# The last output half of a decode kernel, summed as 16 rows of 128 columns

## The chip, the cores and the metric

The kernel runs on one core of a Trainium2 chip. The metric is the device time of one execution in microseconds (us), lower is better. Before the change three runs took 1340.95, 1341.06 and 1341.16 us; the median is 1341.06.

## The reference

One decode step for 4 sequences: attention over a cache of 8192 positions with 32 heads of 128, its output projection, a gated feed-forward part, and a gate that mixes the two. With one position per sequence and one chosen row, what is computed is this:

```python
g = sigmoid((x * gate_w).sum(-1))
q = (x @ wq).reshape(4, 32, 128)
p = softmax(einsum("bhd,bhkd->bhk", q, k_cache) * 128 ** -0.5)
a = einsum("bhk,bhkd->bhd", p, v_cache).reshape(4, 4096) @ wo
y = ((silu(x @ w_gate) * (x @ w_up)) @ w_down) * sigmoid(x @ w_r)
b = x + y
out = g * a + (1 - g) * b
```

The caches hold 4 x 32 x 8192 x 128 bf16 values each; `wo` is 4096 x 1024, and `out` is 4 x 1024 in bf16. Everything that the change touches belongs to `... @ wo` and the sum with `(1 - g) * b`.

## The kernel before

All inputs stream through one ring of SBUF (`flat`), loaded by DMAs that SP issues in the order of the program. The order of the stages is written out by hand (`order` and the loop behind it): the query projection, then the gate and up projections beside the first K loads, then pairs of K and V steps (32 each, four heads a step), with a softmax per group of eight steps. PE, DVE and POOL keep the order of the program; each waits on semaphores and nothing overtakes on its engine.

When the last K step is done, the PSUM space of the scores is freed and two banks `acc0` and `acc1` are opened in it: the two halves of the output, 512 columns each. `acc(0)` is partitions 0 to 3 of the first, `acc(1)` partitions 32 to 35 of the second. `mm_acc` (L296) adds a product to one of them. The down projection (`wd_piece`) and `x` times its weight (`add_x`, an f32 matmul with the 4x4 diagonal `dg`) go in first, and the output projection last.

The output projection takes `wo` in eight blocks `g` of 512 rows; a block lies on 128 partitions with `FR` = 4 rows each, so a block is 4 x 2 matmuls (row `r`, half `n`), each with `LT[:, r, g, :]` (128x4) as weights and 512 columns of `wo` streaming. `LT` is the attention output, turned by `o_rows` (matmuls with an identity, L428, and a DVE copy, L430): blocks 0 to 5 ahead of the last V step, blocks 6 and 7 behind it. `wo_two` and `wo_block` issue the loads of `wo` on SP and return the function that does the products.

Behind the last V step the list `last` is worked off: blocks 1 and 2, the final sums of that step, block 3, `o_rows` for blocks 6 and 7, then blocks 4, 5, 6, and block 7. Block 7 is loaded in pieces (`cuts`): rows 0 and 1 (512 KB), row 2 (256 KB), row 3's first half and row 3's second half (128 KB each). Then DVE evicts `acc(0)` (L694) and SP stores it (L695); ScalarE evicts `acc(1)` (L696) and stores it from its own queue (L697).

`turned` hands out one of two staging tiles `TB` in turn. `Zt` are two tiles of 128 x 4 x 160 bf16 in which POOL lays the query for the K steps (`spread`); after the last K step nothing uses them. `o_ps` are the two PSUM tiles in which the V steps sum; after the last one they are free. `PB` holds the softmax weights, spread by ScalarE and POOL (L568, L570).

## Time and profile before

| what | value |
|---|---|
| median of three runs | 1341.06 us |
| span of the profiled execution | 1339.2 us |
| PE busy (share of the span) | 1031.3 us (77%) |
| DVE busy | 638.7 us (48%) |
| ACT busy | 57.7 us (4%) |
| POOL busy | 67.0 us (5%) |
| moved by DMA | 576.14 MB, mean 430 GB/s |
| chain that ended last, by engine | DMA 67%, PE 22%, DVE 9% |
| idle time of PE ahead of `acc` matmuls of `wo`, until a load | 2.8 us in four waits |

The span runs from the first instruction of the program to the last on this core; the time of a run holds what lies around it too. A busy share is an average over stages; the chain of waits, followed back from the last instruction, tells which of them set the end in each stage. An engine's name with a q (SPq, ACTq) is its queue issuing DMAs. PE means matmuls, PEld the loading of their weights.

### The profile page before, as it was taken

How to read it: one execution, taken by the hardware profiler on the slowest of the kernel's cores; microseconds unless marked ns; L12 is line 12 of the kernel's file. 1: busy time of each engine (PE TensorE's matmuls, PEld its weight loads, DVE VectorE, ACT ScalarE, POOL GpSimd, SP SyncE). 2: the span in 40 equal slices, each digit the busy share in tenths (PEclk: the TensorE clock that was granted, in tenths of full speed). 3: DMA queues.
4: the chain of work that ended last, by engine and by line, in shares of the span. 5: the costliest groups of instructions: out<-in, count | busy, mean ns of one | idle time of the engine just before them, and what ended most of it. 6: DMA issues, size and time to landing. Idle time of an engine off the chain costs nothing.

```text
span 1339.2 us, 6936 instructions
## 1 busy us (share of the span) xinstructions
PE 1031.3 (77%) x4654; PEld 139.8 (10%) x1486; DVE 638.7 (48%) x385; ACT 57.7 (4%) x58; POOL 67.0 (5%) x174
## 2 busy tenths in 40 slices
PE   2386787887777788777787977777797778687887
PEld 0011000001010010101001110100111011111111
DVE  2285998556553436555352556634345556100001
ACT  0000000100010000100010000100000000110000
POOL 2000000100010000100010000100001000100000
PEclk9697998898888998888889988888998889689999
DMA  9999999999999999999999999999999999999998
GB/s 415 433 437 437 435 437 435 420 438 433 433 435 437 427 433 435 429 438 431 433 431 433 435 439 427 429 433 435 438 430 428 433 429 429 438 429 445 422 422 352
DMA packets 13032, 576.14 MB, mean 430 GB/s; under 512 B 1436, under 2 KB 1700, under 8 KB 1970
## 3 DMA queue, kind: packets, MB, share of 16 engines
q1 hardware_dynamic: 12994, 575.69, 99.6%
q8 instruction: 24, 0.39, 0.1%
q14 instruction: 6, 0.05, 0.0%
q10 hardware_dynamic: 8, 0.00, 0.0%
HBM read 575.68 MB, written 0.01 MB: 430 GB/s over the span
## 4 chain that ended last, share of the span: by engine, by line
DMA 67%; PE 22%; DVE 9%; POOL 0%; ACT 0%; issue 0%; SPq 0%
DMA ring<-in_A_k_cache_dram 53%; PE S_ps L516 15%; DMA ring<-in_A_v_cache_dram 10%; DVE ring L511 9%; PE o_ps L587 5%; DMA ring<-in_B_w_gate_dram 3%; DMA ring<-in_A_wo_dram 2%; PE o_ps L342 1%; POOL PB L570 0%; DVE mx L536 0%; PE led L633 0%; ACT TB L545 0%; PE acc L296 0%; POOL Z L492 0%; PE o_ps L633 0%
## 5 line engine op out<-in xcount | busy, mean ns | idle before, releaser
L511 DVE STREAM_TRANSPOSE ring<-ring 128x2048 uint32<-128x2048 uint32 x256 | 566.5, 2276 | 307.7 <-DMA ring<-in_A_k_cache_dram 307.7
L516 PE MATMUL S_ps<-ring,Z 128*128 128x512 bf16 x2048 | 519.9, 408 | 229.3 <-DVE ring L511 216.1
L587 PE MATMUL o_ps<-ring,PB 128*64 128x512 bf16 x2048 | 457.4, 384 | 35.7 <-DMA ring<-in_A_v_cache_dram 33.3
L516 PEld LDWEIGHTS <-Z 128*128 128x128 bf16 x512 | 53.0, 104 | 683.0 <-issue 683.0
L617 DVE SCALAR_TENSOR_TENSOR OS<-o_ps,mE,OS 128x512 f32<-128x512 f32 x33 | 24.8, 751 | 161.7 <-ACT OS L613 160.2
L587 PEld LDWEIGHTS <-PB 128*64 128x64 bf16 x512 | 56.7, 111 | 428.3 <-issue 427.6
L625 DVE SCALAR_TENSOR_TENSOR OS<-o_ps,mE,OS 128x512 f32<-128x512 f32 x5 | 3.7, 750 | 143.6 <-ACT OS L623 143.6
L492 POOL COPY Z<-qa 32x4 bf16<-32x4 bf16 x128 | 25.8, 201 | 716.7 <-PE S_ps L516 689.6
L570 POOL COPY PB<-PT 32x1024 bf16<-32x1024 bf16 (+3 forms) x23 | 33.4, 1452 | 466.6 <-PE o_ps L587 360.7
L613 ACT ACTIVATE OS<-o_ps,mE 128x512 f32<-128x512 f32 x11 | 7.6, 687 | 671.2 <-PE o_ps L587 671.2
L568 ACT COPY PB<-PT 32x1024 bf16<-32x1024 bf16 (+3 forms) x21 | 30.3, 1444 | 22.4 <-PE o_ps L587 17.4
L545 ACT ACTIVATE TB<-S_ps,mx 128x2048 bf16<-128x2048 f32 x4 | 7.9, 1967 | 321.7 <-DVE mx L542 321.7
L254 PE MATMUL S_ps<-identb,x 6*128 6x6 bf16 x8 | 0.6, 196 | 22.3 <-DMA x<-in_gate_w_dram 22.3
L342 PE MATMUL o_ps<-ring,xw 128*4 128x512 bf16 (+2 forms) x128 | 12.9, 490 | 3.5 <-DMA ring<-in_B_w_gate_dram 3.5
L633 PEld LDWEIGHTS o_ps<-selg,OS 128*128 128x128 f32 x88 | 11.5, 191 | 8.8 <-issue 8.5
L550 DVE STREAM_TRANSPOSE PT<-TB 128x2048 bf16<-128x2048 bf16 x4 | 9.2, 2312 | 6.4 <-ACT TB L545 6.4
L296 PE MATMUL acc<-ring,hT 128*4 128x512 bf16 x54 | 7.9, 466 | 5.5 <-DMA ring<-in_B_w_down_dram 5.5
L536 DVE TENSOR_REDUCE mx<-S_ps 128x1 f32<-128x2048 f32 x4 | 9.1, 2282 | 6.0 <-PE S_ps L516 6.0
L296 PE MATMUL acc<-ring,LT 128*4 128x512 bf16 x64 | 8.8, 378 | 3.3 <-DMA ring<-in_A_wo_dram 2.8
L633 PE MATMUL o_ps<-selg,OS 128*128 128x8 f32 x88 | 10.5, 245 | 0.0
L623 ACT ACTIVATE OS<-o_ps,mE 128x512 f32<-128x512 f32 x5 | 3.4, 687 | 151.2 <-PE o_ps L587 151.2
L256 DVE COPY xw<-S_ps 128x48 bf16<-128x48 bf16 x1 | 0.2, 184 | 17.5 <-PE S_ps L254 17.5
(83 smaller groups left out, 88.4 us busy)
## 6 DMA issues: line engine op xcount, KB each, us to landing
ring<-in_A_v_cache_dram SPq DMA_DIRECT2D x7, 4096.0 KB
ring<-in_A_k_cache_dram SPq DMA_DIRECT2D x6, 4096.0 KB, 33.9
ring<-in_A_v_cache_dram SPq DMA_DIRECT2D x6, 2048.0 KB, 28.9
ring<-in_B_w_gate_dram SPq DMA_DIRECT2D x1, 7168.0 KB
ring<-in_B_w_up_dram SPq DMA_DIRECT2D x1, 7168.0 KB
ring<-in_B_w_down_dram SPq DMA_DIRECT2D x1, 6912.0 KB
ring<-in_A_wo_dram SPq DMA_DIRECT2D x2, 2048.0 KB
ring<-in_A_wo_dram SPq DMA_DIRECT2D x3, 1024.0 KB, 34.5
```

The costliest lines, as they stand in the source:

```text
L296: nc.tensor.matmul(acc(n), lhsT=lhsT, rhs=rhs, start=start, stop=True, skip_group_check=True)
L342: nc.tensor.matmul(ps[32 * k:32 * k + Bn, z, :].rearrange("p (f r) -> p f r", r=FR)[:, :, lo:hi], lhsT=xT[TW * half + t], rhs=rhs, start=( ...
L492: nc.gpsimd.tensor_copy(out=Z[at, :, QP - 1 + QP * q], in_=qa[at, :, h0 + q, b])
L511: nc.vector.transpose(out=kn[:, half], in_=kn[:, half])
L516: nc.tensor.matmul(sps[:, z, :], lhsT=Z[:, 2 * half + e, s:s + P], rhs=T[:, half, 16 * z:16 * z + 16, :, e], start=(t + k + half + e == 0) ...
L536: nc.vector.tensor_reduce(out=mx[:, 0:1], in_=sps[:].rearrange("p z n -> p (z n)"), axis=AX.X, op=ALU.max)
L550: nc.vector.transpose(out=PT[:].rearrange("p j i -> p (j i)"), in_=PTs)
L568: nc.scalar.copy(out=Bv[at, :, :, q, :], in_=Pv[at])
L570: nc.gpsimd.tensor_copy(out=Bv[at, :, :, q, :], in_=Pv[at])
L587: nc.tensor.matmul(o_ps[w // 2][row:row + NM, w % 2, :], lhsT=PB[:, RD * (d % NW) + n, z].rearrange("p w s j -> p (w s j)"), rhs=vn[:, j0 ...
L617: nc.vector.scalar_tensor_tensor(out=OS[:], in0=o_ps[w // 2][:, w % 2, :], scalar=mE[:, w:w + 1], in1=OS[:], op0=ALU.mult, op1=ALU.add)
L633: nc.tensor.matmul(oT, lhsT=OS[:, q * Dh:(q + 1) * Dh], rhs=selg[:, q].rearrange("p t s -> p (t s)"), start=(q == 0), stop=(q == 3), skip_ ...
```

## The change

Three things change.

1. In the last block (7), the second output half is not added to `acc(1)` as one matmul of 4 x 512, but as four of 16 x 128 into a new place `fine`: partitions 0 to 15 of `o_ps[0]`, 128 columns. Row 4s + b of `fine` holds columns 128s to 128s + 127 of the half for sequence b. The weights for it are padded: `LP` has, for every row and every s, 128x16 weights that are zero but for the four columns of `LT` at 4s. What `acc(1)` has gathered up to block 6 is brought over by `acc_to_fine`: ScalarE copies it to SBUF as f32, and four f32 matmuls with padded 4x16 identities (`EP`) put it into `fine`. `LP` and `EP` lie in the two `Zt` tiles, which POOL clears again (`fine_weights`).
2. Block 7 is cut in another way: rows 0 and 1; the first half of rows 2 and 3; the second half of row 2; the second half of row 3. The first half is thus complete two pieces before the end.
3. The ends change engines: ScalarE evicts the first half and stores it from its queue; DVE evicts `fine` (16x128), and SP stores it, with the columns put back in place by the store's pattern.

```diff
+    SEG = P
+    NS = NB // SEG
+    SW = NS * Bn
...
         nc.vector.tensor_copy(out=LT[:, :, g0:g1, :], in_=lp)
+        if g1 == NWB:
+            nc.vector.tensor_copy(out=LP.rearrange("p r (s q) -> p r s q", s=NS)[:, :, :, 0:Bn],
+                                  in_=LT[:, :, NWB - 1, :].unsqueeze(2).to_broadcast([P, FR, NS, Bn]))
...
-        elif half is None:
+        elif half is not None:
+            cols = slice(half * NB, (half + 1) * NB)
+            nc.sync.dma_start(out=w[:, r0:r1, cols], in_=wov[:, g, r0:r1, cols])
+        else:
             nc.sync.dma_start(out=w[:, r0:r1].rearrange("p r n -> p (r n)"),
                               in_=wov[:, g, r0:r1].rearrange("p r n -> p (r n)"))
-        else:
-            nc.sync.dma_start(out=w[:, r0, half * NB:(half + 1) * NB], in_=wov[:, g, r0, half * NB:(half + 1) * NB])
...
                 for n in range(NH) if half is None else [half]:
-                    mm_acc(n, LT[:, r, g, :], w[:, r, n * NB:(n + 1) * NB])
+                    if n == 0 or g < NWB - 1:
+                        mm_acc(n, LT[:, r, g, :], w[:, r, n * NB:(n + 1) * NB])
+                        continue
+                    for s in range(NS):
+                        nc.tensor.matmul(fine, lhsT=LP[:, r, SW * s:SW * (s + 1)], rhs=w[:, r, NB + SEG * s:NB + SEG * (s + 1)],
+                                         start=False, stop=True, skip_group_check=True)
         return use
...
+    LP, EP = [z[:].rearrange("p e w -> p (e w)") for z in Zt]
+    LP = LP[:, 0:FR * NS * (SW + Bn)].rearrange("p (r w) -> p r w", r=FR)
+    EP = EP[:, 0:2 * NS * (SW + Bn)].bitcast(F32)
+    fine = o_ps[0][0:SW, 0, 0:SEG]
+
+    def fine_weights():
+
+        for z in Zt:
+            nc.gpsimd.memset(z[:], 0.0)
+        nc.gpsimd.tensor_copy(out=EP[0:Bn].rearrange("p (s q) -> p s q", s=NS)[:, :, 0:Bn],
+                              in_=ident[0:Bn, 0:Bn].unsqueeze(1).to_broadcast([Bn, NS, Bn]))
+
+    def acc_to_fine():
+
+        a = turned(Bn, NB, F32)
+        nc.scalar.copy(out=a, in_=acc(1))
+        for s in range(NS):
+            nc.tensor.matmul(fine, lhsT=EP[0:Bn, SW * s:SW * (s + 1)], rhs=a[:, SEG * s:SEG * (s + 1)],
+                             start=(s == 0), stop=True, skip_group_check=True)
...
                 add_x()
+                fine_weights()
...
-    cuts = [(g, 0, FR) for g in range(4, NWB - 1)] + [(NWB - 1, 0, 2), (NWB - 1, 2, 3)] + [(NWB - 1, FR - 1, FR, n) for n in range(NH)]
+    cuts = [(g, 0, FR) for g in range(4, NWB - 1)] + [(NWB - 1, 0, 2), (NWB - 1, 2, FR, 0), (NWB - 1, 2, 3, 1), (NWB - 1, 3, FR, 1)]
...
-    for use in last:
+    for i, use in enumerate(last):
+        if i == len(last) - 4:
+            acc_to_fine()
         use()
-    res = [turned(Bn, NB, lo=32 * n) for n in range(NH)]
-    nc.vector.tensor_copy(out=res[0], in_=acc(0))
-    nc.sync.dma_start(out=out2[:, 0:NB], in_=res[0])
-    nc.scalar.copy(out=res[1], in_=acc(1))
-    nc.scalar.dma_start(out=out2[:, NB:D], in_=res[1])
+    res = [turned(Bn, NB), turned(SW, SEG)]
+    nc.scalar.copy(out=res[0], in_=acc(0))
+    nc.scalar.dma_start(out=out2[:, 0:NB], in_=res[0])
+    nc.vector.tensor_copy(out=res[1], in_=fine)
+    nc.sync.dma_start(out=out2[:, NB:D].rearrange("b (s c) -> s b c", c=SEG), in_=res[1])
```

## The prediction

> **What bounds the kernel now.** I read the page first, then the chain of waits in order of time for the last 100 us, then the timeline of the last 7 us, and last the groups by shape for prices. The page:

> ```profile
> span 1339.2 us, 6936 instructions
> PEclk9697998898888998888889988888998889689999
> DMA  9999999999999999999999999999999999999998
> ```

> The DMA engines are busy in every slice but a part of the last one, so the loads set the time, and the change moves no byte of them except in how the last 0.5 MB is cut. What it can move is what lies behind the last load. The chain of waits, its end:

> ```profile
> 1311.27 24.05 DMA ring<-in_A_wo_dram
> 1335.32 0.04 issue
> 1335.36 1.05 PE acc L296 x4
> 1336.41 0.02 issue
> 1336.43 0.58 ACT TB L696
> ```

> Up to 1335.32 a load holds the chain, then four matmuls (1.05 us), then ScalarE's eviction of the second half (0.58 us). The timeline of the end (start, length, engine, line, operation, count, idle time before it):

> ```profile
> 1333.46 1.03 PE L296 MATMUL acc<-ring,LT 128*4 128x512 bf16 x8 [1.44 <-DMA ring<-in_A_wo_dram]
> 1334.70 0.60 PE L296 MATMUL acc<-ring,LT 128*4 128x512 bf16 x4 [0.22 <-DMA ring<-in_A_wo_dram]
> ...
> 1335.70 0.69 PE L296 MATMUL acc<-ring,LT 128*4 128x512 bf16 x2
> 1336.12 0.68 DVE L694 CAST TB<-acc 4x512 bf16<-4x512 f32 x1 [6.49 <-PE acc L296]
> 1336.43 0.58 ACT L696 CAST TB<-acc 4x512 bf16<-4x512 f32 x1 [10.90 <-PE acc L296]
> 1336.83 0.29 SPq L695 DMA_DIRECT2D out_dram<-TB  x1
> 1337.04 0.55 ACTq L697 DMA_DIRECT2D out_dram<-TB  x1
> ```

> Block 6 ends at 1334.49 (1333.46 + 1.03). The first cut of block 7 (rows 0 and 1, four matmuls) starts when its load lands, 1334.70; row 2 follows at 1335.36, row 3's first half at 1335.70, its second half at 1336.02 (1335.70 + 0.69 - 0.38), each on landing. PE idles between them: the loads, not PE, hold this end. The span ends at 1339.17, 2.13 us after ScalarE began its store (1337.04).

> **The change, part by part.** All times are on this execution's clock; its span is 1339.2 and the median of the runs 1341.06, so about 1.9 us lie around the span, and I add the change of the span to 1341.06.

> *Prologue of the fine sums.* `fine_weights` puts two memsets and a 4x4x4 copy on POOL behind the spread of the last softmax group. The rows: 625 ns for a memset of Z, some 200 for a copy, 1.45 us in all. POOL finished that spread at 1148.42 and next works at 1177.28 (its timeline), so 27 us of POOL's idle time hide it:

> ```profile
> 1143.54 4.88 POOL L570 COPY PB<-PT 32x768 bf16<-32x768 bf16 x3 [75.46 <-DVE PT L550]
> 1177.28 1.28 POOL L570 COPY PB<-PT 32x256 bf16<-32x256 bf16 x2 [28.86 <-PE o_ps L587]
> ```

> If that cover were gone, the PB copies and with them the V matmuls would be 1.45 us late. The copy of LT into LP is a small DVE operation of 64 elements per lane, about 0.2 us by the 32- and 96-element copies below, after 1329.63; it is wanted after 1335. Nothing on the path.

> *The wait that is added.* `acc_to_fine` stands in PE's order between block 6 and block 7. ScalarE can copy acc(1) only when block 6 is done, and PE can't start the four f32 matmuls before that copy; everything of block 7 is queued behind them on PE, the first half's matmuls too. ScalarE itself has nothing else to do there (10.90 us idle). So: 1334.49 + 0.03 (as from 1336.41 to 1336.43) + 0.58 (row of the same 4x512 shape) + 0.05 (as 1335.32 to 1335.36, and a little for the signal) = 1335.15 at which PE goes on. That is 0.45 us after it goes on now, and the loads no longer hold it.

> *Four f32 matmuls of 128 columns.* The nearest rows:

> ```profile
> L296 PE MATMUL acc<-TB,dg 4*4 4x512 f32 x4 | 1.0, 587 | 0.0
> L355 PE MATMUL S_ps<-identb,TB 128*128 128x128 bf16 x8 | 0.8, 220 | 1.6 <-DVE TB L351 1.3 <-DVE qT L356 0.3
> L360 PE MATMUL S_ps<-qT,R 128*128 128x128 bf16 x4 | 0.5, 260 | 0.3 <-DVE qT L356 0.3
> L430 DVE CAST LT<-led 128x96 bf16<-128x96 f32 x1 | 0.3, 258 | 12.3 <-PE led L428 12.3
> L430 DVE CAST LT<-led 128x32 bf16<-128x32 f32 x1 | 0.2, 191 | 0.9 <-PE led L428 0.9
> ```

> Two f32 multiplications of 512 columns leave four records of 587 ns, in two pairs 0.43 us apart (1.02 in all less 0.59). So a record streams 512 columns in 0.43 us, 128 in 0.107, and a multiplication has two records. Whether the two of a pair were the halves of one multiplication or the two column groups (0:4 and 32:36) this can't tell: 4 x 0.107 = 0.43 us if halves overlap, 8 x 0.107 = 0.86 if not. I take 0.86, since all four now use one column group and a stream can't share it. PE at 1336.01. [...]

> *Block 7's products.* Today each row's two matmuls overlap, being in two column groups (eight in 1.03 us). The fine sums sit on partitions 0 to 15, the group of acc(0), so nothing overlaps any more. A 512-column matmul alone in its group takes 0.215 us (the first row below: 16 in 3.61 us, less one of 0.38, by 15). A weight load and a matmul of 128 columns: four of L355, whose weights are even larger, take 0.40 us in the window below, with 0.22 for one, so 0.06 each; L360's four give 0.08 ((0.5 - 0.26) / 3), the upper end.

> ```profile
> 1321.05 3.61 PE L587 MATMUL o_ps<-ring,PB 128*64 128x512 bf16 x16 [1.28 <-DMA ring<-in_A_v_cache_dram]
> ...
> 31.10:31.50 0.40, 0.40 (x4) 0.28 (x5) 1.00 0.00 0
> ```

> The first cut: 2 x (0.215 + 4 x 0.06) = 0.91, to 1336.92. Rows 2 and 3 of the first half: 0.43, to 1337.35; the last of them began at 1337.13 and is done 0.38 later, at 1337.51. The second half of rows 2 and 3: 8 x 0.06 = 0.48; the last pair starts at 1337.77 and is done 0.22 later, at 1337.99. All the loads are down before, so their new cut (the first half of rows 2 and 3 in 256 pieces of 1 KB, where row 2 was 128 of 2 KB) costs nothing here; a tenth of a us if PE were waiting for it.

> [...]

> *First half out.* ScalarE in place of DVE: 1337.51 + 0.03 + 0.58 = 1338.12, store begun 1338.15, and by today's 2.13 from there the span would end at 1340.28.

> *Second half out.* DVE evicts 16x128 in place of 4x512. From the two L430 rows, 67 ns for 64 elements: 128 elements are 0.29 us, less than today's 0.58 on ScalarE. 1337.99 + 0.03 + 0.29 = 1338.31, store begun by SP at 1338.34. SP's queue has only this store and the closing waits in it. SP's issue is 0.26 us shorter, but its data came as late after the start as ScalarE's (within 0.04 us: pieces up to 1337.73 and up to 1337.98 in the slices of DMA traffic), so 2.09. The store has 16 pieces of 256 B where it had 4 of 1 KB. Today's four begin 0.04 us apart; 12 more at that pace are 0.48, spread over engines that take them side by side 0. I take 0.1, nearer to the lower end, since the first load of the kernel has its sixteen engines begin within 0.3 us (0.02 each). End: 1338.34 + 2.09 + 0.1 = 1340.53.

> *Sum.* 1340.53 - 1339.17 = +1.36 us: PE's last matmul is done 1.59 later (1337.99 against 1336.40), the eviction gives back 0.29, the queue 0.04, the small pieces take 0.1. 1341.06 + 1.36 = 1342.4 us. A measurement of this kernel tells about 0.2% (2.7 us) from no change, so this counts as no change, though slower.

> **The rivals.**

> *Hidden (1340.7).* If PE were through the copy, the f32 sums and the first cut before the last load lands, only the shorter end would remain: 0.29 + 0.04 less 0.1 for the pieces, the final four pairs about as long as the matmul of 0.38 (3 x 0.06 + 0.22 = 0.40). So 0.2 to 0.3 us faster. For it: PE does idle there today. Against it: its idle time between block 6 and row 3's second half is about 0.8 us, and the added work is 0.66 of waiting, 0.86 of f32 and the lost overlap; PE would be ready for the last piece at 1337.59, 1.57 us after it lands (1336.02).

> *f32 halves overlap (1342.0).* All as above with 0.43 for the four matmuls.

> *Small things are dearer (1343.1).* The fine pairs take L360's 0.08 (16 x 0.02 = 0.32) and the 16 pieces of the store 0.48 (0.38 more than taken).

> *The clock falls (slower, 1344.9).* PE would now stand still from 1334.49 to 1335.15. If that cost it the granted clock, all its streams behind the wait (0.86 + 0.91 + 0.43 + 0.48 = 2.68 us) would double, on top of the 1.36: about +4.0, less what no stream is. It decides from 1.3 us more upward. For it: earlier slices show a granted clock of 6 and 7 tenths where PE waits for loads. Against it: the clock of the last windows is 1.00 (column behind the busy times), over an idle time of 1.44 us ahead of 1333.46, longer than this one:

> ```profile
> 1333.00:1334.50 1.50, 1.03 (x8) 0.34 (x8) 0.00 (x0) 0.00 (x0) 0.00 (x0) 1.00 0.68 256
> 1334.50:1335.30 0.80, 0.60 (x4) 0.17 (x4) 0.00 (x0) 0.00 (x0) 0.00 (x0) 1.00 0.50 174
> ```

> That the edit doesn't do what it says hardly arises: PE's order in the built program has the four f32 matmuls behind block 6 and four matmuls per row in place of one.

> **How the numbers follow.** The forecast as summed 0.68 (its own range 1341.9 to 1342.8); f32 overlapping 0.13; small things dearer 0.11; hidden 0.04; the clock 0.04. The range: below, 1341.8 if all low ends come together, and half a us on towards the hidden case where PE had part cover, 1341.3; above, the dear case and 0.2 for the difference between executions, 1343.3. The hidden case is within 0.2%, so faster by more has 0.01; the clock, and an end dearer than any row, make 0.06 slower by more; 0.93 remains for no change.

> **What would show it.** Right: a gap on PE behind block 6 that ScalarE's copy ends; eight f32 records after it, 0.8 to 0.9 us; no later wait of PE for a load; DVE's 16x128 eviction of 0.3 us last in the chain, with the end of the span some 1.4 us later. Wrong: PE waiting for a load at the last cut (hidden), f32 records in overlapping pairs, a granted clock under 1.00 behind 1334, or a span that differs before 1333, which nothing here explains.

## The result, and the profile after

The changed kernel took 1344.71 us (median of nine executions, 1342.92 to 1345.68), the kernel before beside it 1341.20 (1340.95 to 1341.97). The ratio is 1.0022, with a 95% interval of 1.0012 to 1.0031: slower by about 3 us (1.6 to 4.2), where 1342.4 was forecast and 1341.3 to 1343.3 was the range. The nine executions are two groups: four from 1342.92 to 1343.44, five from 1344.71 to 1345.68. The profiled one, 1343.01, is of the lower group, and its span is the page's first line:

```profile
span 1341.0 us, 6980 instructions
```

The end of its chain of waits (start, length, what):

```profile
1301.37 31.93 DMA ring<-in_A_wo_dram
1333.30 0.04 issue
1333.34 1.05 PE acc L300 x8
1334.39 0.02 issue
1334.41 0.58 ACT TB L479
1335.00 0.04 issue
1335.04 1.04 PE o_ps L481 x8
...
1337.48 0.46 PE o_ps L459 x8
1337.94 0.02 issue
1337.97 0.28 DVE TB L732
```

Before, a load held this chain up to 1335.32. Now the last load in it is the one ahead of block 6 (1333.30); from there on it is PE, ScalarE's copy (L479), the f32 matmuls (L481), block 7 and the eviction of `fine` (L732), without a gap. Behind that stand the stores, in the timeline:

```profile
1338.13 0.54 ACTq L731 DMA_DIRECT2D out_dram<-TB  x1
1338.27 0.75 SPq L733 DMA_DIRECT2D out_dram<-TB  x1
```

SP's store of the 16 rows takes 0.75 us to issue, where its store of 4 rows took 0.29. From its start to the end of the span it is 2.7 us (1341.0 - 1338.27).

So the lower group is the forecast with a dearer store. The upper group needed experiments.

### The profile page after: what moved, and what is told of

It reads as the page before. It is cut to its first block, busy times and chain, and to the rows that moved or that the text cites. A ratio compares the mean times of both kernels' runs of the same rounds, so it can differ in the third digit from the quotient of the medians.

```text
span 1341.0 us, 6980 instructions
## 1 busy us (share of the span) xinstructions
PE 1033.3 (77%) x4674; PEld 141.6 (11%) x1506; DVE 638.5 (48%) x386; ACT 58.3 (4%) x59; POOL 68.1 (5%) x177
## 4 chain that ended last, share of the span: by engine, by line
DMA 68%; PE 21%; DVE 10%; ACT 0%; issue 0%; SPq 0%; DVEq 0%
DMA ring<-in_A_k_cache_dram 52%; PE S_ps L549 15%; DVE ring L544 10%; DMA ring<-in_A_v_cache_dram 8%; DMA ring<-in_A_wo_dram 5%; PE o_ps L620 4%; DMA ring<-in_B_w_gate_dram 3%; PE o_ps L346 1%; DVE OS L650 0%; DVE mx L569 0%; ACT TB L578 0%; PE acc L300 0%; PE led L666 0%; PE o_ps L481 0%; PE o_ps L459 0%
```

## The experiments

The lines called "filling products" are `fill(n, g)`: n matmuls of 128x128 by 512 columns over block g's weights of `wo`, already loaded, into a bank of `o_ps[1]` that nothing reads any more.

**1. The changed kernel again**, no edit.

> The changed kernel again, unaltered, for a second profile and more executions. What is open is the spread: nine executions lay between 1342.9 and 1345.7, in two groups near 1343.2 and 1345.0, while the profiled one of 1343.0 is explained to 0.2 us by its end (PE done 1.5 later, store 0.6 dearer). Theory A (clock): in some executions TensorE runs its last 2.7 us of streams at half the granted clock; then a profile of a 1345 execution shows a granted clock of 0.5 behind 1334 and matmuls of 16x128 0.107 us apart in place of 0.056. Theory B (loads): in some executions the last load lands 1 to 2 us later; then block 6 starts near 1335 in place of 1333.3 and the distance from there to the end of the span stays 7.7 us. Both expect the two groups again.

Seven executions, 1343.18 to 1346.41, five of them over 1345; and this time the profile fell on one of the upper group. Its chain:

```profile
1333.78 1.04 PE acc L300 x8
...
1334.85 0.58 ACT TB L479
1335.43 0.04 issue
1335.47 1.88 PE o_ps L481 x8
...
1340.01 0.87 PE o_ps L459 x8
1340.87 0.02 issue
1340.90 0.28 DVE TB L732
```

Its windows (stretch, length, busy time of PE, PEld, DVE, ACT, POOL, granted clock, DMA share, GB/s):

```profile
1333.70:1335.20 1.50, 1.03 (x8) 0.27 (x7) 0.00 (x0) 0.35 (x1) 0.00 (x0) 1.00 0.69 241
...
1335.40:1337.40 2.00, 1.93 (x9) 1.08 (x10) 0.00 (x0) 0.02 (x1) 0.00 (x0) 0.50 0.02 7
```

Up to 1335.43 it is the other profile, 0.44 later. Then the clock is 0.50 and the streams take 1.8 to 1.9 times as long: eight f32 records 1.88 us where they took 1.04, the last eight pairs 0.87 where they took 0.46. From the restart of PE to its last result it is 5.40 us (1340.87 - 1335.47) in place of 2.90. That is theory A; the loads (theory B) give 0.44 us of the difference in span of 2.9.

**2. TensorE kept busy where it waits.**

```diff
     for i, use in enumerate(last):
         if i == len(last) - 4:
             acc_to_fine()
         use()
+        if i == 0:
+            fill(3, 4)
+        if i == 1:
+            fill(6, 5)
...
         nc.scalar.copy(out=a, in_=acc(1))
+        fill(3, 6)
```

> The changed kernel with TensorE kept busy where it waits at the end: 3 products of 128x128 by 512 columns behind block 4, 6 behind block 5, 3 while ScalarE copies acc(1), all into a PSUM bank that nothing reads any more (0.22 us each at full clock, so 0.65, 1.3 and 0.65 us, inside the idle times of 1.0, 1.4 and 0.66). Theory A (clock): the upper group vanishes, median 1343.0 to 1343.4. Theory B (loads): the two groups stay, median 1344 to 1345.

Median 1343.15, ratio 1.0015 (1.0006 to 1.0024). Ten executions lie between 1342.82 and 1343.33 and one at 1344.32; a single one of 3614 us is like nothing else in this study and is left aside. The upper group is gone, but for the one at 1344.32, although PE has more to do.

**3. Without the transfer.**

```diff
-        if i == len(last) - 4:
-            acc_to_fine()
...
-                                         start=False, stop=True, skip_group_check=True)
+                                         start=(r == 0 and s == 0), stop=True, skip_group_check=True)
```

> The changed kernel without the transfer of acc(1): ScalarE's copy and the four f32 matmuls are left out, so the second half holds block 7's product alone. PE then goes on with block 7 as its loads land. My sum: the wait and the f32 matmuls cost 0.66 + 0.86 us on the path, of which some 0.4 comes back as waiting for the last load; PE done at about 1336.6 on the clock of the profile, span 1.3 us shorter than the changed kernel's, 1341.7 us. Theory A (clock) expects the spread to shrink to under 1 us, since little streaming is left behind the last load. Theory B expects the spread of 2.7 us unchanged.

Median 1342.50; nine of eleven executions from 1342.29 to 1342.75 and two long ones, 1343.66 and 1345.63. The long ones are rarer than in the changed kernel, but theory A's spread of under 1 us did not come, and no profile shows a long one of this kernel. PE was done where the sum had it, at 1336.63:

```profile
1336.17 0.46 PE o_ps L459 x8
```

DVE's eviction began at 1336.66; but the store, begun at 1336.96, was not through until 3.4 us later. The DMA view of that stretch has one packet that is not the program's (queue, packets, MB, share of 16 engines):

```profile
q14 instruction: 1, 0.01, 0.7%
```

A fetch of instructions, 8 KB and 0.49 us by its record, ran on a DMA engine from 1338.37. Twelve pieces of the store began from 1338.37 to 1338.47, the last four only at 1338.86, as the fetch ended. The records don't name the DMA engine; that the four waited for the fetch is read from these times, in one profile. The end came 0.7 us later than in the sum, and the misprice is the store's, not PE's.

**4. The stores on each other's queue.**

```diff
-    nc.scalar.dma_start(out=out2[:, 0:NB], in_=res[0])
+    nc.sync.dma_start(out=out2[:, 0:NB], in_=res[0])
...
-    nc.sync.dma_start(out=out2[:, NB:D].rearrange("b (s c) -> s b c", c=SEG), in_=res[1])
+    nc.scalar.dma_start(out=out2[:, NB:D].rearrange("b (s c) -> s b c", c=SEG), in_=res[1])
```

> The changed kernel with the two stores on each other's queue: SP stores the first half (4 pieces of 1 KB), ScalarE's queue the second (16 pieces of 256 B). The 16-piece store took SP 0.75 us to issue where 4 pieces took 0.29, and its data began 1.39 us behind the start of the issue in place of 0.77. If the number of pieces sets that (0.04 us each), ScalarE's issue grows by the same 0.46 (0.55 to about 1.0) and the time stays within 0.3 us or grows by that; if it is SP's queue, which has closing waits behind it, the time falls by 0.6 us. The spread is not touched by this under either theory.

Median 1345.02 with both groups (three executions from 1343.06 to 1343.59, five from 1344.57). The timeline of its end:

```profile
1340.36 0.30 SPq L731 DMA_DIRECT2D out_dram<-TB  x1
1340.92 1.22 ACTq L733 DMA_DIRECT2D out_dram<-TB  x1
```

The dear issue went with the 16-row store: 1.22 us on ScalarE's queue, 0.68 more than its 4-row store had taken there (0.54). So it is not SP that is dear.

**5. The kernel before, kept busy behind blocks 4 and 5** (3 and 6 filling products).

> The kernel before, with 3 and 6 products of 128x128 by 512 columns put into TensorE's idle time behind blocks 4 and 5, into a PSUM bank that nothing reads any more. Of 28 executions of the kernel before, 6 took 1341.5 to 1342.3 where the rest lay at 1340.8 to 1341.3. If TensorE's clock at the end is the cause there too, those executions vanish (all within 1340.8 to 1341.4) and the median stays at 1341.1. If they come from elsewhere in the kernel, about one in five stays above 1341.4. If the products come in the way of block 5 or 6, the median rises by up to 0.3 us.

Median 1341.09 beside 1341.13, eleven executions from 1340.83 to 1341.46. Beside it, 10 of 33 executions of the unaltered kernel before took 1341.70 or more. So what costs the changed kernel 2 to 3 us seems to cost the kernel before up to 1 us. It is an inference from the counts: no profile fell on a long execution of the kernel before, and experiments 6 and 7, measured beside this one without filling products, have only one long execution of eleven each (1341.87 and 1341.95).

**6. The kernel before with 16 pieces in the second half's store.**

```diff
-    res = [turned(Bn, NB, lo=32 * n) for n in range(NH)]
+    res = [turned(Bn, NB, lo=0), turned(Bn, 2 * NB, lo=32).rearrange("p (s c) -> p s c", s=4)[:, :, 0:P]]
...
-    nc.scalar.copy(out=res[1], in_=acc(1))
-    nc.scalar.dma_start(out=out2[:, NB:D], in_=res[1])
+    nc.scalar.copy(out=res[1], in_=acc(1).rearrange("p (s c) -> p s c", s=4))
+    nc.scalar.dma_start(out=out2[:, NB:D].rearrange("b (s c) -> b s c", s=4), in_=res[1])
```

> The kernel before with the second half's eviction and store alone altered: ScalarE lays it out as 4 runs of 128 columns with gaps, so that its store is 16 pieces of 256 B in place of 4 of 1 KB. If the number of pieces sets the issue time, ScalarE's store takes 1.2 us to issue in place of 0.55 (it took 1.22 in the last set) and the time grows by 0.6 to 0.7 us, to 1341.7. If the dearness came from the 16 partitions, or from the engine, it stays at 1341.1.

1341.13 beside 1341.13. Its store, by its line (duration in ns, least, median, most):

```profile
L697 ACTq DMA_DIRECT2D out_dram<-TB x1: 564/564/564, 1337.1 to 1337.1; - x1
```

16 pieces of 256 B, and the issue takes what 4 pieces of 1 KB took (551). So neither the number nor the size of the pieces is dear, and my bound of "12 more at 0.04 us" in the prediction rested on the wrong thing.

**7. The kernel before with the new cuts, engines and queues, without fine sums.** The edit is the second and third part of the change; DVE evicts `acc(1)` as 4x512.

> The kernel before with the second and third part of the change alone: block 7's first half is loaded ahead of the second, ScalarE evicts and stores the first half, DVE evicts the second (4x512, 0.68 us) and SP stores it. No fine sums, no transfer. By the rows: the last matmul is done when it was, the eviction is 0.10 longer, the store 0.04 shorter, so +0.06 us: 1341.1, no difference that can be measured. The transfer theory (wait, f32 matmuls, lost overlap) and the store's pieces then carry all of the loss. The rival: the two 1 KB-piece loads in place of one of 2 KB pieces, or the first half's store beside the last load, make the last load later: +0.2 or more.

1341.17 beside 1341.13, ratio 0.9999 (0.9990 to 1.0007): these parts cost nothing.

**8. The transfer behind the first half's products**, with the filling products of experiment 5.

```diff
-                                         start=False, stop=True, skip_group_check=True)
+                                         start=(r == 0 and s == 0), stop=True, skip_group_check=True)
...
-        for s in range(NS):
-            nc.tensor.matmul(fine, lhsT=EP[0:Bn, SW * s:SW * (s + 1)], rhs=a[:, SEG * s:SEG * (s + 1)],
-                             start=(s == 0), stop=True, skip_group_check=True)
+        def bring():
+            for s in range(NS):
+                nc.tensor.matmul(fine, lhsT=EP[0:Bn, SW * s:SW * (s + 1)], rhs=a[:, SEG * s:SEG * (s + 1)],
+                                 start=False, stop=True, skip_group_check=True)
+        return bring
...
         if i == len(last) - 4:
-            acc_to_fine()
+            bring = acc_to_fine()
+        if i == len(last) - 2:
+            bring()
         use()
```

> The changed kernel with TensorE kept busy behind blocks 4 and 5 as before (clock out of play), and with the four f32 matmuls moved behind the first half's last product: ScalarE copies acc(1) while PE already works on block 7. The wait (0.66 us) is off the path, the f32 streams (0.87) stay on it. By the rows PE starts block 7 at landing, 1334.70, and is done 0.88 + 0.43 + 0.87 + 0.45 + 0.17 later, at 1337.5 where the changed kernel at full clock has 1337.9 to 1338.1: -0.5 us, 1342.6. If the copy's wait were hidden anyway, the time stays at the 1343.1 of the filled kernel.

1342.91: 0.14 below the filled kernel with the early transfer (experiment 10, 1343.05), where 0.5 was expected. In the chain PE goes on with block 7 when its load lands, and the f32 sums stand later:

```profile
1334.65 0.38 PE acc L300
...
1336.12 0.97 PE o_ps L482 x8
1337.09 0.56 PE o_ps L459 x8
```

PE is done at 1337.65, 0.28 earlier than in experiment 10 (1337.93). My sum gave PE 2.80 us from the landing of block 7's load; it took 3.00: the f32 records 0.97 where I had 0.87, and they began 0.09 later than the sum had them (1336.05 in the timeline for 1335.96). Beside experiment 3, which has neither wait nor f32 matmuls, PE needs 1.07 us more behind that landing (3.00 against 1.93). Taking the wait off the path gains 0.28, the f32 matmuls left on it cost 1.07: they are the larger part.

**9 and 10. Which idle time costs the clock?** The filling products only in the added wait (9), or only behind blocks 4 and 5 (10), as in the diff of experiment 2.

> The changed kernel with the three filling products only in the wait that it added (while ScalarE copies acc(1)), none behind blocks 4 and 5. If the added standstill of 0.66 us is what costs the clock, the upper group (1344.5 to 1346.5) vanishes as with all the filling products, median 1343.1. If the clock is lost to the idle time ahead of block 6 (1.0 and 1.4 us behind blocks 4 and 5), which the kernel before has too, the two groups stay, with a median over 1344, and a slow profile shows the clock at 0.5 from about 1335.3.

> The counterpart: the filling products only behind blocks 4 and 5, the added wait as idle as in the changed kernel. If the idle time ahead of block 6 loses the clock, one group near 1343.1. If the added standstill does, two groups as in the changed kernel.

With the wait filled, nine of eleven executions lay at 1342.90 to 1343.44 and two at 1344.68 and 1346.87; with the idle time ahead of block 6 filled, all eleven at 1342.93 to 1343.59. In the unfilled kernel (the result, experiments 1, 4 and 11, which alter only the store or the order of its rows) 19 of 34 lay above 1344. So neither reading was right alone: filling the earlier idle time ends the loss, and filling the wait seems to make it rarer (2 of 11; experiment 11, measured beside it, has 4 of 10, so the counts alone don't settle that). The profile of 9 fell on its execution of 1346.87; windows as in experiment 1:

```profile
1332.00:1333.70 1.70, 0.28 (x4) 0.15 (x5) 0.00 (x0) 0.00 (x0) 0.00 (x0) 1.00 0.75 286
1333.80:1335.00 1.20, 1.20 (x6) 0.20 (x3) 0.00 (x0) 0.00 (x0) 0.00 (x0) 0.50 0.62 219
```

Here the clock fell while block 6 was running, before the added wait began: PE had been busy for 0.28 of the 1.70 us before. This idle time the kernel before has as well.

The clock records say where the clock falls. In all fourteen traces every complete stretch at 0.50 lasts 3.41 us or a multiple of it, so the clock changes in them only at times that lie on a grid of 3.41 us (in the profile of before 67 changes, in the one after 69, all within 0.003 us of it); where the grid lies against the program differs from trace to trace (the last change stands at 1339.88 before and at 1340.94 after). In the four profiles that lost the clock (experiments 1, 4, 9 and 11) it fell at 1335.38, 1335.15, 1333.75 and 1333.31, and in the 3.41 us ahead of that PE was busy for 1.41, 1.36, 1.36 and 1.52 us. In the profiles without filling products that kept it, the least busy stretch of the grid between 1322 and PE's last product had 1.52 (experiment 7) to 1.96 us (experiment 6). Experiment 1 and, below it, the profile after:

```profile
1331.96:1335.38 3.42, 1.41 (x12) 0.35 (x8) 0.00 (x0) 0.53 (x1) 0.00 (x0) 1.00 0.72 267
1330.70:1334.11 3.41, 1.80 (x16) 0.61 (x15) 0.00 (x0) 0.00 (x0) 0.00 (x0) 1.00 0.75 292
```

The two sets meet at 1.52 us, a share of 0.45. An estimate from this: if the grid may lie anywhere along PE's records from 1322 on, a stretch under 0.45 ends ahead of PE's last half us in 46% of its positions in the changed kernel, in 25% when the wait is filled, in 25% in the kernel before, and in none of the kernels with filling products behind blocks 4 and 5. Measured are 19 of 34 above 1344, 2 of 11 (experiment 9), 25 of 112 above 1341.46, and with those filling products 1 of 33 above 1344 (experiments 2, 8, 10) and 0 of 22 above 1341.46 (5, 12). So, by this estimate, both idle times count, each in the executions whose grid takes it in; the 0.45 is read off these same profiles.

**11. The 16 rows in another order** (4b + s), so that the store walks the output upwards.

```diff
-    LP = LP[:, 0:FR * NS * (SW + Bn)].rearrange("p (r w) -> p r w", r=FR)
+    LP = LP[:, 0:FR * NS * (SW + 1)].rearrange("p (r w) -> p r w", r=FR)
...
-    nc.sync.dma_start(out=out2[:, NB:D].rearrange("b (s c) -> s b c", c=SEG), in_=res[1])
+    nc.sync.dma_start(out=out2[:, NB:D].rearrange("b (s c) -> b s c", c=SEG), in_=res[1])
```

> The changed kernel with the 16 rows of the fine sums in another order: row 4b + s in place of 4s + b (other paddings, same matmuls), so that the store walks the output in rising addresses. The 16-row store took SP 0.75 us to issue and its data began 1.39 us behind the start of the issue; 16 pieces of 256 B from 4 partitions took ScalarE 0.56 and 0.80. If the order of the addresses is what is dear, the issue falls to about 0.3 us; if it is the 16 partitions that go to a pattern of two steps, it stays at 0.75. The two groups stay in either case.

SP's issue stays at 0.76 us; 1343.38 with both groups (six executions up to 1343.49, four from 1344.61). The order of the addresses is not it. What is left, by elimination, is that 16 partitions of SBUF go to a pattern of two steps in memory; the two were not tried apart. The profile of before had such a DMA all along: the two loads of `wd_apart` bring rows of a two-step pattern to 12 partitions, and SP's issue of them is

```profile
L411 SPq DMA_DIRECT2D ring<-in_B_w_down_dram x2: 713/786/859, 1113.2 to 1114.1; - x2
```

against 328 ns for a plain load of 128 partitions (L442). Why such a pattern is dear was not tried.

**12. Experiment 5 again.**

> The kernel before with the filling products behind blocks 4 and 5 once more, unaltered, for the number of executions: of 88 executions of the kernel before beside the earlier sets 21 lay above 1341.46 us, of 11 with the filling products none. If the clock at the end is what makes these, again none (one at most) of some 11 lies above 1341.5, and the median stays within 0.1 us of the kernel before's. If the first set was luck, two or three do.

1340.94 beside 1341.08; eleven executions from 1340.76 to 1341.20, none long. With experiment 5, none of 22 lies above 1341.46; of the 112 of the kernel before measured beside all these runs 25 do (2 of 9, 6 of 28, 10 of 33, 5 of 27, 2 of 15). By the ratio, 0.9998 (0.9989 to 1.0007) both times, no difference from the kernel before is measured; what is gone is its long executions.

## Why the prediction was wrong, by its own steps

- *That the wait moves the bound to PE*: right. 1334.39 to 1335.04 is 0.65 us of standstill (0.66 forecast), and no load is waited for behind it. Block 7's first record begins at 1336.01, behind the f32 records; without the transfer (experiment 3) it began at 1334.70, when its load had landed.
- *Four f32 matmuls 0.86 us*: 0.97 from their first record to block 7's first (1335.04 to 1336.01). The eight records start 0.11 apart, one after the other, so the halves don't overlap; that rival falls. The first half's products in one column group follow each other too: its last two start 0.216 apart, where block 6's, in two groups, start in twos 0.004 apart, every 0.215.
- *Block 7*: 0.88 for the first cut (0.91), 0.43 for the first half of rows 2 and 3 (0.43), 0.45 for the last eight pairs (0.48). A pair takes 0.056 us, in rows of at most eight, so the upper bound from L360 was not needed. PE's last result, 1337.94 against 1337.99, is closer than the terms: block 6 ended 0.10 earlier in this execution (1334.39 for 1334.49), which hides that the f32 matmuls took 0.11 more.
- *DVE's eviction 0.29*: 0.28.
- *The new cuts and the exchange of engines cost nothing*: right (experiment 7: 1341.17 beside 1341.13; there PE does wait for these loads, and block 7's products take 1.72 us from first to last in place of 1.69).
- *The store, 2.09 + 0.1*: mis-sized. It took 2.7, so 0.5 us were missing. I took the number of pieces for the cause; experiment 6 shows that pieces cost nothing, and experiments 4 and 11 that the cost goes with the 16-row store on either queue and in either order of rows. The nearest row, L411, stood in the profile and the sum doesn't use it.
- Together: +1.36 forecast, +1.8 in the profiled execution, and 1343.05 to 1343.15 against 1341.09 with the clock held (experiments 10 and 2): +2.0, which is inside the range. The rival *small things are dearer* named just this time, 1343.1, but by luck: its pairs of 0.08 us and its dear pieces were not there.
- *The clock doesn't fall (0.04)*: this is the step that failed. The rival's price was right: 2.68 us of streams doubled, and experiment 1 has PE's stretch 2.50 us longer. Its chance was not: 19 of 34 executions. That its time, 1344.9, is the median within 0.2 is luck: five of these nine were long, and with four of ten the same work has a median of 1343.38 (experiment 11). The argument against it was one execution, in which the clock stood at 1.00 over an idle time of 1.44 us. It did stand there in that one. The kernel before seems to lose it too, in about one execution of four or five by the counts, and its own spread (1340.95 to 1341.16 in three) was too short to show that. What the change did is to let PE work for 2.9 us behind the added wait, all in one column group, where 1.05 us of work stood behind the last load before. That work is exposed to a loss that was there already, and by the estimate under experiments 9 and 10 the added standstill makes the loss about twice as frequent.

## What to carry to other kernels

Work moved behind the last load is paid at the clock that TensorE has there, and after a stretch of waiting for loads that was 0.50 of full speed in some executions here and 1.00 in others (experiment 1's profile and the one after; 19 of 34 executions above 1344 us): price it at both, and count executions before trusting one profile. A few products into an unused bank while TensorE waited held the clock here (one of 33 executions above 1344 us with them, experiments 2, 8 and 10), and cost nothing that was measured (experiments 5 and 12, both 0.9998), since the idle time was there anyway. The shorter last eviction was worth less than what was done to prepare it: 0.3 us of eviction against 2.0 of transfer, lost overlap and store.
